# Half-width pairs: letting 128-column matmuls join the column tiling of their neighbours, with a new hand-searched order

## The chip, the cores and the metric

The kernel runs on one core of one Trainium2 chip. The core has a matmul engine (TensorE, "PE" in the profile; its weight loads stand apart as "PEld"), VectorE (DVE), ScalarE (ACT), GpSimd (POOL), and SyncE (SP), which here issues DMAs. Matmuls write to PSUM, eight banks of 128 partitions by 512 float32. The metric is the device time of one launch in microseconds (us). Times of the kernel before are the median of three runs.

## The reference, cut to what matters

Two identical layers, each an attention with a recurrent memory followed by a gated feed-forward net (FFN). Sizes: 2048 tokens of width 576, 32 heads of 128, segments of 32 tokens, 8 memory tokens, FFN width 4608. All in bfloat16.

```python
def _A_ref(x, mem0, Wq, Wk, Wv, Wo, seg_len):
    ...
    for s in range(n_seg):                       # 64 segments, in sequence
        xs = x[:, s * seg_len:(s + 1) * seg_len, :].copy()
        h = jnp.concatenate([mem, xs], axis=1)   # 8 + 32 = 40 rows
        q = jnp.einsum('btd,dhe->bhte', h, Wq)
        k = jnp.einsum('btd,dhe->bhte', h, Wk)
        v = jnp.einsum('btd,dhe->bhte', h, Wv)
        scores = jnp.einsum('bhqe,bhke->bhqk', q, k) * scale
        scores = jnp.where(mask[None, None], scores, -1000000000.0)
        p = _softmax(scores, axis=-1)
        o = jnp.einsum('bhqk,bhke->bhqe', p, v)
        o = jnp.einsum('bhte,hed->btd', o, Wo)
        mem = o[:, :M, :].copy()                 # the next segment needs it
        outs.append(o[:, M:, :])
...
x = x + _A_ref(_layernorm(x, axis=-1), A_mem0, A_Wq, A_Wk, A_Wv, A_Wo, A_seg_len)
x = x + _B_ref(_layernorm(x, axis=-1), B_w1, B_w3, B_w2)   # silu(x w1) * (x w3), then w2
x = x + _A_ref(_layernorm(x, axis=-1), A_mem0, A_Wq, A_Wk, A_Wv, A_Wo, A_seg_len)
x = x + _B_ref(_layernorm(x, axis=-1), B_w1, B_w3, B_w2)
```

The memory makes the 64 segments of a layer a chain: a segment's keys and queries cannot be computed until the output projection of the segment before is done.

## The kernel before, in words

**Steps.** The second layer's weights are the first's, so the kernel runs both layers at once, the second eight segments behind (`LAG`). A step `t` handles segment `t` of layer 0 and `t-8` of layer 1, 80 rows in all; there are 72 steps, and in the first and the last few only one layer is there (40 rows). Wq, Wk, Wv and Wo stay in SBUF (`W`, `WV`, `WO`); the FFN's weights are streamed for each group of four segments through small buffers (`W13`, `W2C`), 18 "pairs" of 256 FFN columns per group. At the end W and WV are no longer needed, and the last group's FFN weights are loaded straight into them (`tail_load`).

**Nodes and letters.** `make_nodes` describes the whole program as nodes: an engine, an assumed duration, dependencies, and slots of buffer pools that it takes and gives back. The order of the PE nodes is written out by hand as a string with one letter per node (`FIRST`, then `FOUR` eleven times, each for four steps, then `LAST`). The letters: Q and q are the projection to q and k and its remainder (576 = 4 x 128 + 64; lower case is always the 64-row remainder), S the scores, T the transposes of the probabilities (matmuls against an identity), P probabilities times V, O and o the output projection and the remaining 64 of its 576 columns, V, X, G (v, x, g) the passes that make V for memory rows, for segment rows, and for both kinds of rows in 128 columns, F and f the FFN's first half, W and w its second half for layer 0 and layer 1, and m, a, b, n, p transposes around the layer norms and residuals.

**The plan.** `plan` walks through that string and gives the instructions of the other engines their order by assumed durations: a node starts when its engine, its inputs and its slots are free; ACT and DVE share the "AD" nodes (PSUM copies), the first free takes one. The order in each queue is fixed then; the chip waits on semaphores.

**Tilings of the PE array.** Each PE node has a `mode`. "full" uses the array as one of 128 rows by 128 columns. "row" splits it in two of 64 rows (q, f, g: two remainders side by side). "col" splits it in two of 64 columns (S of two layers, o). "c32", "oct" and "quad" split it in 32-column strips, those by 64 rows, and four quarters (V, X and v, x). In `plan` every change of mode between neighbours in the string costs the assumed `SWITCH` = 0.098 us. The emitter writes matmuls through `mm` (line 580 of the profile), ACT operations through line 583, DVE's through line 586, and SP's DMAs through line 589, so all PE groups in the profile bear L580.

Of the kernel before, what the change touches and what calls it, by code (L numbers as in the profile page):

```python
# [13 lines left out]
P = 128  # L14
R64 = 64
# [36 lines left out]
class Node:  # L52
# [3 lines left out]
    def __init__(self, eng, dur, fn, deps=(), prio=0.0, mode=None, acq=(), rel=(), name="", lat=None):  # L56
        self.eng, self.dur, self.fn, self.prio, self.mode = eng, dur, fn, prio, mode
        self.deps = [d for d in deps if d is not None]
        self.acq, self.rel, self.name = list(acq), list(rel), name
        self.lat = lat if lat is not None else (PE_LAT if eng == "PE" else EW_LAT)  # L60
        self.outs, self.ready, self.start, self.end, self.by = [], 0.0, None, None, None
        self.left = len(self.deps)
# [13 lines left out]
def plan(nodes, pools, letters):  # L76
# [16 lines left out]
    mode = None  # L93
    order = []
    at = 0
# [18 lines left out]
    while len(order) < len(nodes):  # L114
        best = None
        for e in t_eng:
            if e == "PE":
                cands = seq[at:at + 1] if at < len(seq) and seq[at].left == 0 else []
            else:
                cands = ready[e] + (both if e in ("ACT", "DVE") else [])  # L120
            if not cands:
                continue
            ests = [(est(e, n), n) for n in cands]
            t = min(x for x, _ in ests)
            if t >= NOW:
                continue
            if best is None or t < best[0]:
                best = (t, e, ests)
        if best is None:
            raise RuntimeError(f"the plan is stuck at {at}: {seq[at].name}")  # L130
        t, e, ests = best
        st, n = min((x for x in ests if x[0] <= t + 1e-9), key=lambda x: x[1].prio)
        dur = n.dur
        if isinstance(dur, tuple):
            dur = dur[0] if e == "ACT" else dur[1]
        if e == "PE":
            at += 1
            if n.mode != mode:
                dur += SWITCH
                mode = n.mode  # L140
        elif n.eng == "AD":
            both.remove(n)
        else:
            ready[e].remove(n)
        n.start, n.end, n.by = st, st + dur, e
        t_eng[e] = n.end
        for s in n.acq:
            if s.i is not None:
                continue
            f = free[s.pool]  # L150
            s.i = min((i for i in range(len(f)) if f[i] <= st + 1e-9), key=lambda i: f[i])
            f[s.i] = NOW
        for s in n.rel:
            s.users -= 1
            s.end = max(s.end, n.end + (PE_LAT if e == "PE" else EW_LAT))
            if s.users == 0:
                free[s.pool][s.i] = s.end
        for m in n.outs:
            m.ready = max(m.ready, n.end + (0.0 if m.eng == e == "PE" else n.lat))
            m.left -= 1  # L160
            if m.left == 0:
                push(m)
        order.append(n)
    return order
# [20 lines left out]
def ewh(*ns):  # L185
# [5 lines left out]
    "maQqqqQQSQqqqQTQSqqQSQSXVxvPTPTOPOTOoooPOoQQQqqVSqqvQQqqSQQqqSQTXPSxTOPTPOTOPoooOoaQQqqqqQSvQVSqQQqTQSqqQSPTPOOT"  # L191
    "ooPTPOOooQQqqqvqSVQQQqSTQqqQPSqQOSoTXPTOPTOPxooOoQQpQqqqqQSVSnvqQFffqFQQTSqqPQOToSfFPWTOPfFTOPFOfoooWQQfqqqQSvVF"
    "qfQFQWSqqQFSfQTQPqqfFOTSoWPFTOPfxXTFPOOoooWQQqqfqQQSfqFSvVfqqQFQWSqTQQPFqffTOSoPWOTFPFTOPfaOoooWQFQqqfQSVvqqfFQQ"
    "SqWQQqqqQSTPSTbOPoXTOPTxxPOOoooXqqQpQQqqSVvnQFFSfqQqfqQQTSqfFPQTOPSofWTOPFOTFPWOoooFQqqffQQqSQQQqqgqGTSWPQQfqqFF"
    "fgSSTGGPFgfTOWPOfgGTOPFOooooWQQfqqqFQvSfqFQQfqSVTFQqfFQPSaTWQPfqqFOSoTWFOPffFTOPWOoooFQqqqfQQSWQqqQQSqqTbQSGgqgQ"
    "PGTGPSggOTGPOTOPoooOoQQppqqVqqvSQQnnQFSfqfqFTQQPFSqqfQTwOPWFSoffTOFPwTOPWOoooFQffqqFQwWSQQFfqqfFTGqqgSQPQFWTQSgf"
    "qqGQwPFTSfggOGGPOTwPOOooooWFfqqQQFQqfqvVSQQWFfqqSQwTFPaSqfqQTQwFWPSffTOPFOOTwPWOooooFqqfqQQWqSQQQSqqqQQbQSqggGTG"
    "PGTSggPGTOPOTwPOOoooo"
)
FOUR = (  # L200
    "QqQpQpQqqqvVSSnnQFffqqFQQTFSffqqQPFTWSPOwTFPOTOPwOooooWQQqqqfQSQQQqqqfFGgfSSTFPFQqfqgGQTWwPFTSfggGFPGOTOPOOooooW"
    "wQQqqqfQFQvfqfVSSwFQWQFqffqFWTQPwTFSffqqQOPWoSwTFPFOTOPwWOoooffFQqqQWQSqqqQaQSbQQTQqqqgGSSgPGTGPOTggGPOTwPOOoooo"
)
LAST = (
    "QQpqqqQpSqqQQnVqvSnQTQQPqqSFTSffOPFOTFPfwTOPFOooooWQQqfqqQFwWSfqfQQFGSgfqqQTFPGwSTWFqfgqQQPWTFSfgfgGFwGPOTOPOOoo"
    "oofFWQwQFqfqqQQWSfqVvSQFTFqqfQPQTwSqqfFOQPWwffSFTFPOOTFPWOoooowQQqqqfQQSvqqqVSQWTQQPqqQOTSSbPwvVoXTOPToxPOOooVpp"
    "qqvQQQqqSQQnnQqqfSFQTFPSfqqQTFfSPOOwTWPFfTOPFOoooowQWfqqQQQFvqqfVSSFQQfqqFTWQfqqSQPwTOPoSXfTFPOWOTxfPFOwoooFQQvq"
    "fqVSqqQQWwFTQqfqfSQQPFwFqfqSQTWOPSfFTFWPOTOPwOooooffQFqqQWQSqqqQwFvSfVQTQPWqqQSOQqwTSbPOTXoPToxPOOooQqqqqQpQQSVv"
    "QnqSQFqfqfFQTQqSPSwTOPFFTffoPOTOPwOoooFQqqfqQQqfvSVFQFQSqfqQTQQqfqSFPSXTwPOTFPOTxooPOOoowQQqqvfSVqqqQQQSqQQTSfFP"
    "FTfqqQOoSPwTfOFPFTOPfooOowQQqqqqQSQQSqfqFQVvSfFTwQQqfqPTSFPFTOPOTOPwOooooffpFnwFfffFFFwffFFwfffFFwFwfffFFFwfffFF"  # L210
    "wFwFffffFFww"
# [11 lines left out]
def make_nodes(em, nseg, pools, o=Opt, dma_bw=230e3, load_bw=400e3):  # L223
# [44 lines left out]
    def ln_nodes(tag, src, xn, deps, prio, writes, warm=False):  # L268
# [5 lines left out]
        d = node("PE", 5 * 0.056, em.ln_tr(xn, b, warm), deps=[c], prio=prio, mode="full", acq=[b], rel=[xn], name=tag + "tr")  # L274
# [26 lines left out]
    def v_nodes(name, t, k, prio, tail_at, emit, strips, deps, tail_deps, free):  # L301
# [6 lines left out]
        for r in (0, 1):  # L308
            outs = em.v_parts(strips, r)
            b[r].users = len(outs)  # L310
            for p0, width, row, blk in outs:
                e = node("AD", ew(512), em.v_ev(b[r], p0, width, row, blk), deps=[m_, n] + free.get(blk // 2, []), prio=prio + 0.01 * (blk // 2),
                         rel=[b[r]], name=name + "e")
                vx_ev.setdefault((name, t, blk // 2), []).append(e)
# [6 lines left out]
    def vg_nodes(t, g, deps, tail_deps):  # L321
# [4 lines left out]
        m_ = node("PE", 8 * 0.2158, em.vg(t, g, b, False), deps=deps, prio=t + o.vm, mode="full", acq=b, name="VG")  # L326
# [5 lines left out]
    def vg_out(t, g, b, deps, row):  # L332

        return [node("AD", ew(512), em.v_ev(b[r], row, R64, row, 2 * g + r), deps=deps, prio=t + o.vm + 0.01 * g + (0.05 if row == 0 else 0.0), rel=[b[r]],
# [11 lines left out]
    def step(t):  # L346
# [17 lines left out]
        for g in range(NG):  # L364
# [18 lines left out]
            sc = node("PE", 8 * 0.0165 * nl, em.scores(t, g, qs, s), deps=qe, prio=pf + o.sc, mode="col", acq=[s, sme], rel=qs, name="SC")  # L383
# [9 lines left out]
            tr = node("PE", 8 * mm80, em.ptr(t, g, pb, bt), deps=[pbs], prio=pf + o.tr, mode="full", acq=[pts] + bt, name="TR")  # L393
            node("POOL", 1.2, em.pb_zero(pb), deps=[tr], prio=pf, rel=[pb], name="pbz")
            pe_ = [node("AD", ew(4 * c80), em.pt_ev(t, g, m, bt[m], pts), deps=[tr], prio=pf, rel=[bt[m]], name="PTe") for m in (0, 1)]
            if paired(t):
# [6 lines left out]
                      prio=pf + o.pv, mode="full", acq=b + [ot], rel=[pts], name="PV")  # L403
# [14 lines left out]
        if t == nst - 1:  # L418
            last_reads[2].extend(wos)
# [14 lines left out]
    def post(li, g):  # L434
# [4 lines left out]
                 prio=prio, mode="full", acq=b, name="POST")  # L439
# [3 lines left out]
    last_reads = [], [], []  # L443
    kept = {}

    def job(j):
# [18 lines left out]
        if last:  # L465
            v_done, qk_done, wo_done = last_reads
            tail = []
            for i in range(8):
                late = wo_done[i - 4:i - 3] if i >= 4 else []
                parts = [(0, 9 * 512, qk_done[2 * i:2 * i + 2] + late), (1, 4 * 576, v_done + late)]  # L470
                tail.append([load("tail", kb(128, c), s0 + o.tail_at + 0.01 * i, em.tail_load(i, what), deps=dep) for what, c, dep in parts])

        npp = NPR // 2
        for at, pp in enumerate([npp - 1] + list(range(npp - 1)) if last else range(npp)):
            mids, w2s, htts, lds = [], [], [], []
            stays = last and pp == npp - 1
            for pr_ in (2 * pp, 2 * pp + 1):
# [18 lines left out]
                fm = node("PE", 16 * mm, em.ffn_up(ents, pr_, w13, b, last and not stays, False), deps=wr + ld, prio=prio, mode="full",  # L496
# [8 lines left out]
            for (bi, g) in ents:  # L505
                b = banks()
                d = node("PE", 8 * 0.1225, em.ffn_down(bi, pp, htts, w2s, b, last and not stays), deps=mids + lds, prio=prio + o.w2,
                         mode="full", acq=b, rel=htts + w2s, name="W2b" if bi else "W2")
# [52 lines left out]
class Emitter:  # L561


    def __init__(self, nc, tc, T, aps, nseg):
# [4 lines left out]
        self.tail_w, self.ys = {}, {}  # L569
# [9 lines left out]
    def mm(self, out, lhsT, rhs, start, stop, **k):  # L579
        self.ch("PE", self.nc.tensor.matmul(out, lhsT=lhsT, rhs=rhs, start=start, stop=stop, skip_group_check=True, **k))  # L580
# [113 lines left out]
    def tail_load(self, i, what):  # L694

        def f(n):
            T = self.T
            fa = i * 512
            t13, t2 = T.W[:, :, fa:fa + 512], T.WV[:, i * 4 * D:(i + 1) * 4 * D].rearrange("p (b d) -> p b d", b=4)
            if what != 1:  # L700
                for kind, wd in ((0, self.a.w1), (1, self.a.w3)):
                    self.dma(t13[:, 4 * kind:4 * kind + 4], wd[0:4 * P, fa:fa + 512].rearrange("(c p) f -> p c f", p=P))
                for kind, wd in ((0, self.a.w1), (1, self.a.w3)):
                    self.dma(t13[kind * R64:(kind + 1) * R64, 8], wd[4 * P:D, fa:fa + 512])
            if what != 0:
                self.dma(t2, self.a.w2[fa:fa + 512, :].rearrange("(b p) d -> p b d", p=P))
            for h in range(2):
                self.tail_w[2 * i + h] = (t13[:, :, h * 2 * P:(h + 1) * 2 * P], t2[:, 2 * h:2 * h + 2])
# [219 lines left out]
    def scores(self, t, g, qs, s):  # L928

        def f(n):  # L930
            S = self.bk(s)[:, 0:GH * QW].rearrange("p (h k) -> p h k", h=GH)
            both = self.both(t)
            for hl in range(4):
                for ab in (0, 1):
                    Q = self.T.QKT[:, qs[ab].i].rearrange("p a h n -> p (a h n)")
                    for kd in ((0, 1) if both else (0,)):
# [3 lines left out]
                                True, True, tile_position=(0, 64 * kd))  # L940
# [249 lines left out]
def kernel(  # L1190
# [88 lines left out]
    for n in plan(nodes, pools, ORDER):  # L1279
        n.fn(n)  # L1280
# [35 lines left out]
```

## Time and profile before

| what | value |
|---|---|
| median of 3 runs | 2701.53 us (2697.99 to 2702.61) |
| the profiled execution's own time | 2696.12 us |
| its span, first to last instruction | 2694.4 us |
| granted TensorE clock | 0.995 of full speed |
| PE busy | 98% of the span, 55,795 matmuls |
| DVE / ACT / POOL busy | 78% / 51% / 12% |
| DMA | 321 MB, 119 GB/s on average |

The profile's matmuls are pipelined: one matmul's record lasts about 0.2 us, but the next may start 0.036 us after it, so PE counts as busy even when little is done. What an operation costs is therefore read from starts: from the start of its first matmul to the start of the first matmul of whatever follows. In a timeline, the columns are the start in us, the length of a merged group in us, the engine and line, the operation, its output and inputs, its shape and the number of instructions. "128\*64" ahead of a shape means 128 rows and 64 columns of weights; "128\*128" is the full array.

### The profile page before, as it was taken

The numbers are of one execution on the slowest core, as the hardware profiler recorded it, in microseconds if no ns is written. First come the engines' busy times: TensorE is split into PE (matmuls) and PEld (weight loads), VectorE is DVE, ScalarE is ACT, GpSimd is POOL, SyncE is SP. The second block draws the span as 40 slices with busy tenths as digits, with TensorE's granted clock in tenths as the row PEclk, the third lists the DMA queues.
The fourth block names the chain that finished last, engine by engine and source line by source line (L and its number), as shares of the span: only waits on it lengthen the run. The fifth ranks groups of instructions, "written<-read, shape, count | busy, mean of one in ns | idle before, by whom it ended". The sixth has DMA issues, their size and how long they took to land.

```text
span 2694.4 us, 126628 instructions
## 1 busy us (share of the span) xinstructions
PE 2635.1 (98%) x55795; PEld 2225.2 (83%) x55795; DVE 2088.9 (78%) x5376; ACT 1366.8 (51%) x4025; POOL 333.2 (12%) x400
## 2 busy tenths in 40 slices
PE   5999999999999999999999999999999999999998
PEld 4788888888888888888888888888888888888886
DVE  4777887878778777777877777787787777787876
ACT  2655554545545454554545445464544546454453
POOL 1111110111101011010101101010110101011110
PEclk8999999999999999999999999999999999999999
DMA  9064524234342423434243343433334342434458
GB/s 317 8 188 126 159 79 120 81 110 119 108 134 71 126 84 110 124 106 131 76 119 89 110 126 97 129 88 114 94 110 126 92 133 71 125 97 135 119 161 263
DMA packets 483065, 321.42 MB, mean 119 GB/s; under 512 B 26344, under 2 KB 477296, under 8 KB 481872
## 3 DMA queue, kind: packets, MB, share of 16 engines
q1 hardware_dynamic: 478976, 305.44, 38.5%
q8 instruction: 437, 7.16, 1.1%
q0 software_dynamic: 3024, 6.93, 0.9%
q10 hardware_dynamic: 512, 0.94, 0.1%
q14 instruction: 116, 0.95, 0.1%
HBM read 308.49 MB, written 2.36 MB: 115 GB/s over the span
## 4 chain that ended last, share of the span: by engine, by line
PE 88%; ACT 4%; DMA 3%; DVE 3%; issue 1%; SPq 0%; ACTq 0%; POOL 0%; DVEq 0%; POOLq 0%
PE bank L580 88%; ACT V L583 3%; DMA W<-in_B_w_dram 2%; DVE SME L586 1%; DMA W<-in_A_Wk_dram 1%; DVE STAT L586 1%; DVE V L586 1%; ACT SME L583 0%; DMA WV<-in_A_Wv_dram 0%; ACT XTB L583 0%; ACT QKT L583 0%; ACT PTS L583 0%; SPq L589 0%; DVE PB L586 0%; DVE OT L586 0%
## 5 line engine op out<-in xcount | busy, mean ns | idle before, releaser
L580 PEld LDWEIGHTS <-W 128*128 128x128 bf16 (+1 forms) x29520 | 1237.5, 98 | 141.9 <-issue 44.3
L580 PE MATMUL bank<-HT,W 128*128 128x80 bf16 (+3 forms) x23040 | 810.9, 196 | 17.0 <-ACT HT L583 6.3
L580 PE MATMUL bank<-XTB,W 128*128 128x256 bf16 (+3 forms) x6480 | 660.9, 261 | 6.7 <-DMA W<-in_B_w_dram 5.9
L583 ACT ACTIVATE QKT<-bank 128x256 bf16<-128x256 f32 (+3 forms) x1587 | 365.9, 317 | 369.1 <-PE bank L580 350.0
L995 POOL MEMSET PB<- 128x1024 bf16 x288 | 273.9, 951 | 1809.8 <-PE bank L580 1312.3
L580 PE MATMUL bank<-OT,WO 128*128 128x80 bf16 (+3 forms) x11520 | 406.8, 198 | 0.8 <-DVE OT L586 0.5
L583 ACT ACTIVATE V<-bank 64x512 bf16<-64x512 f32 (+1 forms) x616 | 346.4, 584 | 105.9 <-PE bank L580 100.6
L580 PEld LDWEIGHTS <-WO 128*128 128x128 bf16 (+1 forms) x11520 | 379.4, 102 | 15.9 <-issue 5.8
L580 PE MATMUL bank<-WV,HT 128*32 128x512 bf16 (+4 forms) x3240 | 367.5, 383 | 1.0 <-issue 0.7
L580 PE MATMUL bank<-W2C,HTT 128*128 128x288 bf16 x2240 | 315.1, 286 | 0.0
L586 DVE TENSOR_TENSOR PB<-SME,STAT 40x128 bf16<-40x128 f32 (+4 forms) x912 | 275.2, 336 | 14.9
L586 DVE TENSOR_REDUCE STAT<-SME 104x8 f32<-104x320 f32 (+1 forms) x576 | 273.5, 475 | 14.5 <-ACT SME L583 9.3
L583 ACT ACTIVATE HTT<-bank 128x512 bf16<-128x512 f32 (+1 forms) x324 | 179.7, 556 | 181.8 <-PE bank L580 179.8
L580 PEld LDWEIGHTS <-HT 128*32 128x32 bf16 (+4 forms) x3240 | 136.9, 96 | 152.3 <-issue 33.4
L586 DVE SCALAR_TENSOR_TENSOR XR<-bank,XR 128x288 f32<-128x288 f32 x576 | 246.2, 449 | 16.0 <-PE bank L580 8.0
L580 PEld LDWEIGHTS <-HTT 128*128 128x128 bf16 x2304 | 209.7, 98 | 48.5 <-DVE HTT L586 0.3
L583 ACT ACTIVATE OT<-bank 128x320 bf16<-128x320 f32 (+1 forms) x399 | 149.5, 404 | 166.1 <-PE bank L580 165.0
L586 DVE CAST QKT<-bank 128x192 bf16<-128x192 f32 (+2 forms) x461 | 124.7, 316 | 134.3 <-PE bank L580 133.0
L586 DVE SCALAR_TENSOR_TENSOR HTT<-HTT,bank 128x512 bf16<-128x512 bf16 (+1 forms) x324 | 202.1, 624 | 33.7 <-ACT HTT L583 29.7
L586 DVE TENSOR_TENSOR HTT<-HTT,bank 128x512 bf16<-128x512 bf16 (+1 forms) x324 | 203.4, 628 | 30.7 <-DVE HTT L586 0.5
L583 ACT ACTIVATE PTS<-bank 128x320 bf16<-128x320 f32 (+1 forms) x384 | 144.1, 402 | 163.4 <-PE bank L580 126.7
L583 ACT ACTIVATE SME<-SME 104x320 f32<-104x320 f32 (+1 forms) x288 | 135.4, 470 | 138.3 <-DVE SME L586 135.6
(61 smaller groups left out, 1803.3 us busy)
## 6 DMA issues: line engine op xcount, KB each, us to landing
W<-in_B_w_dram SPq DMA_DIRECT2D x612, 256.0 KB, 3.5
W2C<-in_B_w_dram SPq DMA_DIRECT2D x306, 288.0 KB, 3.3
W<-in_B_w_dram SPq DMA_DIRECT2D x612, 32.0 KB, 3.4
W<-in_B_w_dram SPq DMA_DIRECT2D x16, 512.0 KB, 8.8
W<-in_A_Wq_dram SPq DMA_DIRECT2D x9, 512.0 KB, 9.0
WO<-in_A_Wo_dram SPq DMA_DIRECT2D x4, 1152.0 KB, 15.3
XR<-in_A_x_dram POOLq DMA_DIRECT2D x16, 288.0 KB, 2.9
WV<-in_B_w_dram SPq DMA_DIRECT2D x8, 576.0 KB, 7.1
```

The source lines that it names most:

```text
L580: self.ch("PE", self.nc.tensor.matmul(out, lhsT=lhsT, rhs=rhs, start=start, stop=stop, skip_group_check=True, **k))
L583: self.ch("ACT", self.nc.scalar.activation(*a, **k))
L586: self.ch("DVE", getattr(self.nc.vector, fn_)(*a, **k))
L995: return lambda n: self.ch("POOL", self.nc.gpsimd.memset(self.T.PB[:, pb.i], 0.0))
```

## The change

**Modes become lists.** A node may name several modes ("full/col"). FFN (F, W, w), the 128-column V passes (G), the transposes (T, p, n, a, b) and P may run in either; Q, O and m stay "full"; the scores of a single layer, which need only 40 columns, may also be either. While the planner walks along the string it keeps the modes that all nodes since the last change have in common, and changes only when the next node shares none of them. The run of nodes then takes the first mode that is left (`settle`): "full" unless a neighbour in the run is only "col".

**Pairs.** In mode "col", `mm` splits a 128-column matmul into two of 64 columns, at column 0 and column 64 of the array, each with the same moving operand.

**The assumed costs** of copying V out of PSUM and of a single layer's scores are new constants.

**The tail's loads.** The last group's FFN weights come in four loads of 1024 FFN columns instead of eight of 512, and the later ones no longer wait for output projections.

**The order strings** `FIRST`, `FOUR` and `LAST` are all new, of the same letters and lengths.

```diff
-        self.eng, self.dur, self.fn, self.prio, self.mode = eng, dur, fn, prio, mode
+        self.eng, self.dur, self.fn, self.prio, self.mode = eng, dur, fn, prio, mode.split("/") if mode else mode
...
-    mode = None
+    mode, run = [], []
...
+    def settle():
+        for x in run:
+            x.mode = mode[0]
+        run.clear()
...
-            if n.mode != mode:
+            if not any(m in mode for m in n.mode):
                 dur += SWITCH
+                settle()
                 mode = n.mode
+            mode = [m for m in mode if m in n.mode]
+            run.append(n)
...
-            sc = node("PE", 8 * 0.0165 * nl, em.scores(t, g, qs, s), deps=qe, prio=pf + o.sc, mode="col", acq=[s, sme], rel=qs, name="SC")
+            sc = node("PE", 8 * (0.0165 * nl if nl == 2 else 0.029), em.scores(t, g, qs, s), deps=qe, prio=pf + o.sc, mode="col" if nl == 2 else "full/col", acq=[s, sme], rel=qs, name="SC")
...
-        m_ = node("PE", 8 * 0.2158, em.vg(t, g, b, False), deps=deps, prio=t + o.vm, mode="full", acq=b, name="VG")
+        m_ = node("PE", 8 * 0.2158, em.vg(t, g, b, False), deps=deps, prio=t + o.vm, mode="full/col", acq=b, name="VG")
...
(the same for the nodes TR, PV, FF, W2, POST and the layer norms' transposes)
...
-            for i in range(8):
-                late = wo_done[i - 4:i - 3] if i >= 4 else []
-                parts = [(0, 9 * 512, qk_done[2 * i:2 * i + 2] + late), (1, 4 * 576, v_done + late)]
-                tail.append([load("tail", kb(128, c), s0 + o.tail_at + 0.01 * i, em.tail_load(i, what), deps=dep) for what, c, dep in parts])
+            for i in range(4):
+                parts = [(0, 9 * 1024, qk_done[4 * i:4 * i + 4]), (1, 8 * 576, v_done)]
+                tail += [[load("tail", kb(128, c), s0 + o.tail_at + 0.01 * i, em.tail_load(i, what), deps=dep) for what, c, dep in parts]] * 2
...
     def mm(self, out, lhsT, rhs, start, stop, **k):
+        if self.mode == "col" and "tile_position" not in k:
+            for r in (0, R64):
+                self.mm(out[r:r + R64], lhsT[:, r:r + R64], rhs, start, stop, tile_position=(0, r), **k)
+            return
         self.ch("PE", self.nc.tensor.matmul(out, lhsT=lhsT, rhs=rhs, start=start, stop=stop, skip_group_check=True, **k))
...
     for n in plan(nodes, pools, ORDER):
+        em.mode = n.mode
         n.fn(n)
```

## The prediction

> **What bounds the kernel now.** I read the page first.
>
> ```profile
> PE 2635.1 (98%) x55795; PEld 2225.2 (83%) x55795; DVE 2088.9 (78%) x5376; ACT 1366.8 (51%) x4025; POOL 333.2 (12%) x400
> PEclk8999999999999999999999999999999999999999
> PE 88%; ACT 4%; DMA 3%; DVE 3%; issue 1%; SPq 0%; ACTq 0%; POOL 0%; DVEq 0%; POOLq 0%
> ```
>
> PE carries the chain; the rest sits mostly at the two ends, where weights arrive. "98% busy" does not say what the time goes to, so I read the PE timeline for starts.
>
> ```profile
> 1107.11 1.15 PE L580 MATMUL bank<-W2C,HTT 128*128 128x288 bf16 x8
> 1108.18 0.34 PE L580 MATMUL bank<-OT,WO 128*64 128x80 bf16 x8
> 1108.35 0.41 PE L580 MATMUL bank<-QKT 128*64 128x40 bf16 x16
> 1108.69 0.54 PE L580 MATMUL bank<-W2C,HTT 128*128 128x288 bf16 x3
> ```
>
> Full tiling, then column tiling (o and S), then full again. W2 took 1.07 from its start to o's. Where no change of tiling follows, it takes 0.98:
>
> ```profile
> 1503.71 1.15 PE L580 MATMUL bank<-W2C,HTT 128*128 128x288 bf16 x8
> 1504.69 2.00 PE L580 MATMUL bank<-OT,WO 128*128 128x80 bf16 x64
> 1506.63 1.15 PE L580 MATMUL bank<-W2C,HTT 128*128 128x288 bf16 x8
> ```
>
> So a change cost 0.09 here. Over all the trace's starts, from the last matmul of one tiling to the first of another, it is 0.132 to 0.134 after an 80-column matmul (0.036 without a change) and 0.202 to 0.205 after a 256-column one (0.109 without): 0.093 to 0.098, I take **0.097**. Walking the order string with the rule for modes, the kernel before changes tiling 1,294 times, or 125 us. By the same starts some 2,465 us are matmuls at their full rate. The rest is waiting: about 2.5 us in each 200 us of the middle, but some 31 us in the first 100 us and 14 in the last 95.
>
> **Part 1, changes of tiling removed.** One turn of `FOUR`, a bar for each change, before and after:
>
> ```
> |Q|q|QpQpQ|qqq|v|V|SS|nnQF|ffqq|FQQTF|S|ffqq|QPFTW|S|POwTFPOTOPwO|oooo|WQQ|qqqf|Q|S|QQQ|qqqf|FG|gf|SS|TFPFQ|qfqg|GQTWwPFT|S|fgg|GFPGOTOPOO|oooo|WwQQ|qqqf|QFQ|v|fqf|V|SS|wFQWQF|qffq|FWTQPwTF|S|ffqq|QOPW|oS|wTFPFOTOPwWO|ooo|ff|FQ|qq|QWQ|S|qqq|QaQ|S|bQQTQ|qqqg|G|SS|g|PGTGPOT|gg|GPOTwPOO|oooo
>
> |Q|qq|v|pQQpQ|qq|V|SSnn|QQF|ffqq|FQTQ|qqf|SFPwTWFS|ff|OPFTWPOTOPwO|ooooF|qfqq|QQQWQ|q|wSSFF|ffgq|GQTQPQ|gqqq|GTwS|QPWG|SFT|fgfg|FPGOTOPOwO|ooooF|qffq|QFQWQ|q|S|V|v|QQQ|qqqf|FTWPwSSFF|qffq|QQTOw|SWPFT|ff|FOPWTwPOO|ooooF|qqfq|QQQWQ|S|qqq|aQ|S|QQbQ|gqq|SGTSGP|g|TGPOT|gg|GPOTOPwO|oooo
> ```
>
> That is 65 against 57, eleven times; `FIRST` goes from 320 to 274, `LAST` from 259 to 209. Together 1,294 to 1,110: 184 fewer. Eight of them lie where loads set the pace (six in step 0, two in the tail after the last p), so 176 x 0.097 = **-17.1 us** on the path. Nothing else runs on PE at a change, so nothing hides it.
>
> **Part 2, the pairs.** By the same walk 166 of 324 F, 104 of 288 W and w, 43 of 108 G, 62 P, 89 T and 30 transposes become pairs: 5,190 added matmuls, each with a weight load. If a pair costs what the one matmul did, this is free; 17.1 us over 5,190 pairs is 3.3 ns, so that is the margin. The trace has pairs of four kinds. At 512 columns, first the full form (8 matmuls), then two-column tiles (8 pairs):
>
> ```profile
> 1455.48 1.89 PE L580 MATMUL bank<-WV,HT 128*128 128x512 bf16 x8
> 1457.21 0.45 PE L580 MATMUL bank<-ident,PB 104*128 104x80 bf16 x8
> ```
>
> ```profile
> 2391.70 1.92 PE L580 MATMUL bank<-WV,HT 128*64 128x512 bf16 x16
> 2393.46 0.40 PE L580 MATMUL bank<-QKT 128*64 128x40 bf16 x16
> ```
>
> 1.73 against 1.76: 4 ns a pair, and by the single starts (0, 240, 456, 671 ns ...) all of it in the first pair. At 80 columns, the 64 matmuls from 1504.69 to 1506.63 above are 32 O and 16 pairs of o: 1.94 - 32 x 0.036 - 2 x 0.097 = 0.60, 37 ns a pair against 36. At 40 columns it is worse, 30 against 25:
>
> ```profile
> 1004.71 0.68 PE L580 MATMUL bank<-QKT 128*64 128x40 bf16 x32
> ```
>
> (0.68 - 0.19 for the last one) / 31 = 16 ns a matmul. Only 17 of the new nodes (8 T, 9 P) are that short: 17 x 8 x 5 ns = +0.7 us. Pairs of 256 and 288 columns the trace doesn't show; they lie between 80 and 512, so 0 to +4 ns each: 3,488 pairs, 0 to +14 us. I take +0.3, for the excess in the rows sits at the first pair of a node. In all **+1**, with ends 0 and +15.
>
> [...]
>
> **Part 3, waits that the new order makes or ends.** PE's queue is in order: a node that waits holds up all behind it. I summed the PE work between each producer and its consumer in `FOUR`, and compared it with the shortest distance that ran without a wait in the trace. Scores to T has 6.35 at least (ran at 5.27), V to P 2.1 (1.8), F to w 5.4 (4.0), T to P and P to O 0.98 as before. Three, once in each turn, are shorter than any seen: o to p 2.07 (2.83 seen), q to S 1.34 (1.74), b to g 1.24 (1.81). What p needs after o:
>
> ```profile
> 1506.76 0.22 ACT L583 ACTIVATE HT<-bank 128x64 bf16<-128x64 f32 x1 [2.56 <-PE bank L580]
> 1507.01 0.23 ACT L583 ACTIVATE YO<-bank 64x80 f32<-64x80 f32 x1
> 1507.28 0.35 DVE L586 TENSOR_TENSOR HT<-bank,YO 64x16 bf16<-64x16 f32 x2 [1.87 <-ACT YO L583]
> 1507.66 0.45 ACT L583 ACTIVATE YTS<-bank 128x128 bf16<-128x128 f32 x2 [0.41 <-DVE HT L586]
> 1508.51 0.28 DVE L586 TENSOR_TENSOR YTS<-bank,YO 64x32 bf16<-64x32 f32 x2
> ```
>
> Done at 1508.79, 2.3 after the last o (1506.53, 0.036 after its last start); 0.4 of that is DVE being elsewhere. So p waits 0 to 0.3, and the other two alike: 33 x (0 to 0.3) = 0 to +10. On the other side, each turn before (157.5 us) holds waits of 0.41 (Q after o, which stays), 0.39 (inside a q) and 0.28 (inside a P); the last two may vanish, 11 x 0.67 = -7. I take **+2** (-7 to +10). DVE, at 78%, keeps its work; 0.5% less time does not make it the bound.
>
> **Part 4, the ends.** The tail waits for weights:
>
> ```profile
> 2678.69 0.84 PE L580 MATMUL bank<-XTB,W 128*128 128x128 bf16 x12 [1.28 <-DMA W<-in_B_w_dram]
> 2684.43 3.83 PE L580 MATMUL bank<-XTB,W 64*128 64x128 bf16 x40 [2.69 <-DMA W<-in_B_w_dram]
> ```
>
> With one of 0.8 at 2685, the excess at these places is 5.1 us. The same bytes now come in 20 DMAs on SP's queue instead of 40, in rows of 2 KB instead of 1 KB, and without waiting for O. At best all waits go: -5. At worst the last load lands when it did (2685.8) and, now holding twice the columns, has 4 F, 4 f and 2 w behind it (6.3 us by rows) where before 4.6 followed: +2. A load of the small W2 buffer waits in the same queue (issued at 2647.7) and still holds back what is behind it. I take **-1.5**. At the start, V's matmuls ended at 44.9; the last of Wv landed at 42.4 and a quarter of them must follow, so at best 43.7: **-1** (0 to -1.2).
>
> **The sum.** -17.1 + 1 + 2 - 1.5 - 1 = -16.6 against the profiled execution's own 2696.1, so 2679.5. That execution was 5.4 us under the median of 2701.5; against the median it is **2684.9**. The ends together, not all at once, give the forecast's own range of 2674 to 2697.
>
> **The rivals.**
>
> *The waits eat it.* The new distances cost 1.5 us a turn instead of 0.2, or the W2 and V copies queue up on ACT and DVE. For it: the order is tuned on assumed durations, and three distances are untested. Against it: the others are as long as before. 11 x 1.5 = 16.5, so about 2699, no change that counts.
>
> *A pair is not one matmul (slower).* One mechanism: with 64-column weight loads, the short pairs (T, P) run at the weight load's pace in longer runs than o's eight. Their place is the 1,208 pairs of T and P; it decides from 14 ns a pair (17 us) on. At 60 ns a pair (24 more) they cost 29 us, so 2684.9 + 29 = 2714. Against it: the o rows, where 16 pairs in a row ran at 37 ns. For it: no row has long columns between short pairs, and a margin of 3.3 ns over all pairs is thin.
>
> *The change isn't made:* the runs fall back to "full". The rule of `settle` counted above leaves 494 pair nodes, so I give this almost nothing (2701).
>
> **Chances.** Forecast 0.82, waits 0.09, pairs 0.08, not made 0.01. What a measurement of this kernel can tell from no change is about 0.2%, or 5.4 us. The forecast lies wholly beyond it but for its upper end (0.01 of it): faster 0.81, same 0.11 (0.09 + 0.01 + 0.01), slower 0.08. The range of 2673 to 2699 takes in the forecast's ends and reaches to the waits' case.
>
> **What would show it.** In the profile after: about 61,000 matmuls; groups of 128\*64 for XTB, W2C, PTS and PB; F nodes in pairs that still take 1.75 us, W2 0.98, T and P 0.29 from start to start; a turn of `FOUR` of some 156.8 us instead of 157.5; the two waits for W in the tail shorter. Wrong would be: pairs of T or P over 50 ns, more than 1 us of new waits a turn before p, S or g, or an end that waits longer for W.

## The result, and the profile after

| | median | ratio to before (95%) |
|---|---|---|
| before, beside it | 2702.07 us (2697.99 to 2704.96, 4 runs) | |
| after | 2691.87 us (2686.26 to 2696.43, 4 runs) | 0.9962 [0.9939, 0.9986] |
| the same kernel again (e1) | 2694.26 us (2686.84 to 2696.46, 9 runs) | 0.9973 [0.9964, 0.9983] |

Faster by 7 to 10 us by the two ratios; the forecast was 16.6. The profiled execution of after took 2696.43 us, near the top of its range, that of before 2696.12, below all its timed runs; so the two traces must be compared stretch by stretch, not by their ends. From after's page:

```profile
PE 2622.5 (97%) x60931; PEld 2286.7 (85%) x60995; DVE 2103.0 (78%) x5463; ACT 1361.9 (51%) x3938; POOL 332.5 (12%) x400
PEclk8999999999999999999999999999999999999999
q8 instruction: 477, 7.82, 1.2%
PE 85%; DVE 7%; DMA 3%; ACT 2%; issue 1%; SPq 1%; POOL 0%; ACTq 0%; DVEq 0%
```

60,995 weight loads are the 55,795 of before, 5,190 of the pairs and 10 of a warm-up node in pairs (64 matmul records are missing in this trace). The third line is what the prediction left out: 477 instruction packets with 7.82 MB, 16.4 KB each. Before had 437 with 7.16 MB.

The pairs in the timeline of after (start, length, group; twice as many matmuls in each):

```profile
1490.58 1.94 PE L591 MATMUL bank<-XTB,W 128*64 128x256 bf16 x32
1492.33 0.48 PE L591 MATMUL bank<-PTS,V 128*64 128x80 bf16 x16
1492.62 1.17 PE L591 MATMUL bank<-W2C,HTT 128*64 128x288 bf16 x16
1493.60 0.48 PE L591 MATMUL bank<-ident,PB 104*64 104x80 bf16 x16
1493.88 1.18 PE L591 MATMUL bank<-W2C,HTT 128*64 128x288 bf16 x16
1494.87 1.94 PE L591 MATMUL bank<-XTB,W 128*64 128x256 bf16 x32
```

From start to start F takes 1.75, P 0.29, W 0.98, T 0.28, W 0.99: what they took in the full array. At these sizes a pair costs what the one matmul did.

Where the time went shows best in four stretches: first Q to the first `FOUR` (FIRST), the eleven turns (middle), from there to the last p (LAST), and the tail to the last matmul. "Pauses" are gaps that end 1.15 to 1.8 us after an instruction packet's landing, where every instruction delivered before it had been used. A packet lands when its 16.4 KB have arrived. All from starts in the traces, us; the kernels e1 to e12 are those of the experiments.

| trace | FIRST | middle | LAST | tail | pauses in FIRST / LAST |
|---|---|---|---|---|---|
| before | 502.0 | 1734.1 | 392.2 | 40.0 | 3.0 / 3.2 |
| after | 508.1 | 1722.8 | 397.0 | 39.6 | 7.3 / 4.8 |
| e1, after again | 504.7 | 1724.9 | 398.1 | 39.4 | 5.9 / 5.9 |
| e5, only the middle changed | 505.2 | 1725.0 | 396.1 | 40.3 | 4.6 / 4.1 |
| e6, only the ends changed | 504.2 | 1737.6 | 399.3 | 38.4 | 4.6 / 7.7 |
| e7, old tail loads | 502.6 | 1723.4 | 397.5 | 39.6 | 5.8 / 5.7 |
| e12, LAST old | 500.2 | 1723.5 | 395.3 | 45.3 | 4.0 / 4.7 |
| e8, before, no repeated loads | 502.0 | 1732.3 | 393.4 | 35.3 | 2.3 / 4.5 |
| e9, ends, no repeated loads | 496.5 | 1733.4 | 402.3 | 35.9 | 0.4 / 7.0 |
| e10, after, no repeated loads | 495.6 | 1720.5 | 402.9 | 36.2 | 1.3 / 8.9 |

The middle gained 9 to 11 us, more than forecast for it. The ends, where I had counted half of the removed changes of tiling, gained nothing.

**Why the ends had fewer changes to remove.** A score of a single layer has weights of 40 columns. The changed kernel calls 62 of the 64 such nodes "full" and gives them no place in the array; I counted no change around them. In the trace of after, and then in that of before, where the same node is called "col":

```profile
154.61 0.37 PE L591 MATMUL bank<-QKT 128*40 128x40 bf16 x8
154.92 0.34 PE L591 MATMUL bank<-HT,W 128*128 128x40 bf16 x7
157.88 0.78 PE L591 MATMUL bank<-HT,W 128*128 128x40 bf16 x25 [2.62 <-issue]
```

```profile
2626.29 0.37 PE L580 MATMUL bank<-QKT 128*40 128x40 bf16 x8
2626.59 0.94 PE L580 MATMUL bank<-HT,W 128*128 128x40 bf16 x31
```

0.31 and 0.30 from the score's first matmul to Q's first. Eight matmuls of the same 40 moving columns with 128-column weights, in e1's trace, take 0.21:

```profile
2616.61 0.35 PE L591 MATMUL bank<-PTS,V 128*128 128x40 bf16 x8 [0.35 <-ACT PTS L594]
2616.82 1.14 PE L591 MATMUL bank<-W2C,HTT 128*128 128x288 bf16 x8
```

So leaving a "full" score still costs a change. So does entering it: from the last matmul of a Q of 40 columns to the first score it is 109 ns in the median in before (20 nodes called col) and 109 in e7 (21 called full), against 25 from one Q to the next. Leaving takes about 111 under either name, so around these scores a change costs some 85 ns. And in the one place where o, which is in two-column tiling, follows a "full" score, there is no such gap: in a further trace of after (span 2688.9 us) the first o starts there at 114.63 us, ahead of the last two scores (114.65). So the gaps go by the width of the weights here, not by the node's name: in the programs that the two kernels build, the 512 matmuls of these scores carry the same tile, 128 rows by 64 columns at column 0, whichever name the node has.

Counted with these scores in column tiling, `FIRST` has 320 changes before and 311 after, the middle 715 and 627, `LAST` 259 and 259: **97 fewer, not 184**, 88 of them in the middle.

**What a pause drags behind it.** The last line of the first of these fences is the other surprise: 2.62 us in the middle of a Q node that waits for no data. It costs more than its length: right behind it the same 20 FFN matmuls take 1.81 us to the next start (first two lines) and 1.10 in e10, where the pause is missing (last two):

```profile
158.50 2.01 PE L591 MATMUL bank<-XTB,W 128*128 128x128 bf16 x20
160.31 0.47 PE L591 MATMUL bank<-HT,W 64*128 64x40 bf16 x16
```

```profile
152.88 1.27 PE L592 MATMUL bank<-XTB,W 128*128 128x128 bf16 x20
153.98 0.36 PE L592 MATMUL bank<-HT,W 64*128 64x40 bf16 x16
```

The further trace of after shows the clock at such a place: 1.00 from 2620 to 2625 us, then a pause (2.34 us for instructions, to 2628.0), a granted clock of 0.50 from 2629.8 to 2640.0 (with a second pause in it, of 1.19) and 1.00 again from 2641 to 2646. Not every pause is followed by it: behind one of 1.84 us (to 211.0) the clock stays at 1.00 in the same trace, behind one of 2.07 us (to 2635.2) in a further trace of before (span 2695.6 us). A stretch of 3.4 us at half clock costs up to 1.7 us, which the table's pauses leave out.

### The profile page after: what moved, and what is told of

Same layout as the page of the kernel before. It is cut to its first block, busy times and chain, and to the rows that moved or that the text cites. A ratio compares the mean times of both kernels' runs of the same rounds, so it can differ in the third digit from the quotient of the medians.

```text
span 2694.7 us, 137011 instructions
## 1 busy us (share of the span) xinstructions
PE 2622.5 (97%) x60931; PEld 2286.7 (85%) x60995; DVE 2103.0 (78%) x5463; ACT 1361.9 (51%) x3938; POOL 332.5 (12%) x400
## 3 DMA queue, kind: packets, MB, share of 16 engines
q1 hardware_dynamic: 474048, 305.43, 38.4%
q8 instruction: 477, 7.82, 1.2%
## 4 chain that ended last, share of the span: by engine, by line
PE 85%; DVE 7%; DMA 3%; ACT 2%; issue 1%; SPq 1%; POOL 0%; ACTq 0%; DVEq 0%
PE bank L591 85%; DVE STAT L597 1%; ACT V L594 1%; DVE SME L597 1%; DVE HTT L597 1%; SPq L600 1%; DMA W<-in_B_w_dram 1%; DVE PB L597 1%; DMA W<-in_A_Wk_dram 1%; DVE V L597 1%; DVE XN L597 0%; DMA WO<-in_A_Wo_dram 0%; DVE LNS L597 0%; DMA XN<-in_A_x_dram 0%; ACT PTS L594 0%
## 5 line engine op out<-in xcount | busy, mean ns | idle before, releaser
L591 PEld LDWEIGHTS <-W 128*128 128x128 bf16 (+2 forms) x32176 | 1267.8, 100 | 130.0 <-issue 62.6
L591 PE MATMUL bank<-XTB,W 128*64 128x256 bf16 (+5 forms) x9136 | 659.3, 263 | 5.6 <-DMA W<-in_B_w_dram 3.7
L594 ACT ACTIVATE QKT<-bank 128x64 bf16<-128x64 f32 (+2 forms) x1500 | 349.7, 312 | 352.7 <-PE bank L591 347.1
L591 PE MATMUL bank<-W2C,HTT 128*64 128x288 bf16 (+1 forms) x3072 | 323.6, 287 | 1.4 <-DMA W2C<-in_B_w_dram 1.0
L591 PEld LDWEIGHTS <-HT 128*32 128x32 bf16 (+5 forms) x3584 | 154.2, 98 | 124.8 <-issue 17.4
L591 PEld LDWEIGHTS <-HTT 128*64 128x64 bf16 (+1 forms) x3136 | 223.7, 105 | 35.7 <-issue 2.4
L594 ACT ACTIVATE OT<-bank 128x320 bf16<-128x320 f32 (+1 forms) x420 | 155.2, 403 | 147.6 <-PE bank L591 144.6
L597 DVE CAST QKT<-bank 128x128 bf16<-128x128 f32 (+4 forms) x548 | 147.6, 316 | 87.9 <-PE bank L591 85.6
## 6 DMA issues: line engine op xcount, KB each, us to landing
W<-in_B_w_dram SPq DMA_DIRECT2D x8, 1024.0 KB, 12.3
```

The lines of the kernel that those rows point to most:

```text
L594: self.ch("ACT", self.nc.scalar.activation(*a, **k))
L597: self.ch("DVE", getattr(self.nc.vector, fn_)(*a, **k))
```

## The experiments

Three theories at first: (A) instructions come late, (B) the new ends wait longer for data, (C) short pairs cost more. That "full" scores change the tiling came out of the traces last.

**e1, the changed kernel again.** No edit.

> The kernel after, unchanged, for a tighter interval and a second profile. Three theories of why the gain was 10 us and not 17. (A) Instructions arrive late: the pairs add 9% to PE's instructions, and where 40-row steps need one matmul per 25 ns PE now and then runs out of them. Then the long pauses inside Q nodes of the first profile (1.1, 2.8 and 2.2 us at 150, 155 and 214 us, 2.5 and 1.4 at 2631 and 2638) move or change length from run to run, each with a packet of PE's instruction queue that starts late, and the times scatter by some 10 us. (B) The new FIRST and LAST wait longer for data: the same waits stand at the same nodes with the same lengths. (C) Short pairs cost more than one matmul: the middle turns lose it, 44 nodes of P and 66 of T. All three: ratio 0.994 to 0.999.

The gain is there again: 2694.26 us, 0.9973. In the table its middle is as in after, and pauses sit at the same stages with other lengths: the Q at 155 us paused 2.6 us in after and 1.7 in e1.

**e2, the new modes on the old strings; e3, the new strings without pairs.**

```diff
 e2: FIRST, FOUR, LAST of before, all else as after
 e3:
-mode.split("/") if mode else mode
+mode.split("/")[:1] if mode else mode
-mode="col" if nl == 2 else "full/col"
+mode="col"
```

> The new modes, pairs, assumed costs and tail loads on the old order strings: 1,210 changes of tiling instead of 1,294, 286 nodes with pairs (or wide V) instead of 498. By the count alone 84 x 0.097 = 8.1 us faster than the kernel before, 2694. (A) fewer added instructions, so less is lost than after: 2692 to 2698. (B) the old strings have the old waits: the whole 8 us, plus or minus the tail. (C) P and T pairs are 84 instead of 151 nodes: a loss of 0.05 us each at their ends would leave 4 us of the gain.

> The new order strings with one mode to a node, as before (everything of 128 columns in full tiling, all scores in column tiling), so no pairs: 1,412 changes of tiling. By the count 118 x 0.097 = 11.4 us slower than the kernel before (2713) and 302 x 0.097 = 29 us slower than the kernel after (2721), as the new strings were made for pairs. (A) PE's instructions are as many as before, so its long pauses are as short as before (about 4 us): nearer to 2710. (B) the waits of the new strings stay, whatever the tiling: 2718 or more. (C) faster than the count by what the pairs cost.

e2: 2723.16 us, ratio 1.0093 [1.0079, 1.0108]. e3: 2742.65 us, 1.0156 [1.0142, 1.0169]. Both far slower than before, and than anything I expected of them. The waits of e3, then of e2:

```profile
PE bank L591 <- ACT V L594: 15.3, 34, 2.1
PE bank L591 <- DVE HTT L597: 7.6, 23, 0.5
PE bank L591 <- DVE PB L597: 7.4, 8, 1.9
```

```profile
PE bank L591 <- ACT V L594: 9.3, 26, 2.9
PE bank L591 <- DVE PB L597: 8.0, 10, 1.8
PE bank L591 <- DMA W2C<-in_B_w_dram: 5.3, 3, 3.9
```

(us in all, times, longest. In before V's row is 5.2 and PB's 1.4, and HTT has none.) A string, its modes and its assumed costs fix the order of every queue together; these rows fit that one without the others queues V's and P's copies in the wrong places. These two say nothing of a change's price, but they show that the parts' worths don't add up.

**e4, pairs for Q and O too.**

```diff
-  ... mode="full", ... name="QK")      (and name="WO")
+  ... mode="full/col", ...
```

> The kernel after with Q and O allowed in column tiling as well: 881 changes of tiling instead of 1,110, and 1,537 nodes with pairs instead of 498, some 25,500 added matmuls instead of 5,190. By the count 229 x 0.097 = 22 us faster than after: 2669. (A) PE's instruction queue must bring 46% more than before, and an 80-column pair uses up four instructions in 36 ns: PE waits for instructions in the middle turns too, and the time is over 2700. (B) nothing new waits: 2670 to 2680, less what the plan's fixed order loses. (C) at 1 ns or more a short pair 20 us or more of the gain go.

2949.47 us, 1.0919 [1.0903, 1.0936]. Its waits, and a Q stretch of its timeline:

```profile
PE bank L591 <- issue: 187.7, 210, 2.7
...
567.34 2.48 PE L591 MATMUL bank<-HT,W 128*64 128x80 bf16 x128 [0.81 <-issue]
571.09 0.81 PE L591 MATMUL bank<-HT,W 128*64 128x80 bf16 x35 [1.26 <-issue]
```

At 80 columns the pairs still run at the single's rate (a Q node of pairs 1.14 to 1.17 us); at 40 they don't (1.14 against 0.81). But 128 matmuls with their 128 weight loads are one packet of 256 instructions; PE used this one up in 2.5 us and then stood for 1.26. C falls at 80 columns, A is real.

**e5, only the middle changed; e6, only the ends; e7, the old tail loads.** Each hybrid takes the strings, modes and V costs of before in the steps named; e5 has the old tail loads, e6 the new.

```diff
 in plan, e5 (e6 without the "not"; with the strings and V costs to match):
+    for i, n in enumerate(seq):
+        if not len(FIRST) <= i < len(FIRST) + 11 * len(FOUR):
+            n.mode = n.mode[:1]
 e7:
-            for i in range(4):
+            for i in range(8):
+                late = wo_done[i - 4:i - 3] if i >= 4 else []
```

> The middle eleven turns as in the changed kernel (order, pairs, assumed copy costs), both ends (FIRST, LAST, the tail's loads) as before; 1,206 changes of tiling against 1,294 and 1,110. Between the two profiled runs the eleven turns gained 11.3 us. If the ends are where the rest of the forecast gain is lost (late instructions there, theory A, or waits for data there, theory B), this kernel keeps all of the 11.3: ratio to before 0.9958, about 2689 us, as fast as the changed kernel or some 3 us faster, with pauses without a data wait summing to about 9 us as before. If the middle's gain only moves a wait from the middle to the last part (rival D), the gain shrinks to under 6 us (ratio over 0.9978).

> The ends (FIRST, LAST, the tail's loads) as in the changed kernel, the eleven middle turns as before; 1,198 changes of tiling, 96 fewer than before, 88 of them on the path. By the price of a change alone: -8.5 us, -1.5 for the tail, -1 for the head, so ratio 0.9959 (2689). Theories A and B: the ends' new order loses what it saves to late instructions (A) or to waits for data (B), so -2 to +4 us, ratio 0.9993 to 1.0015. A shows in the trace as pauses inside nodes with no data wait, summing to 12 to 15 us against 9 before, at other nodes in each execution; B as waits on ACT, DVE or DMA at the same nodes each time, 4 us or more above before's.

> The changed kernel with the tail's weight loads as before: 40 transfers of 1 KB rows instead of 20 of 2 KB, the last four pieces held back until O is done. The prediction's term for this was -1.5 us (bounds -5 to +2), so undoing it should cost +1.5: ratio to the changed kernel 1.0006. By the two profiled runs the tail gained 0.4 us: then no difference (0.9998 to 1.0004). If 2 KB rows keep the queues so busy that instructions come late near the end (A at the tail), undoing it is a gain of 1 to 3 us.

e5: 2690.65 us, 0.9965 [0.9954, 0.9976], as fast as the whole change. e6: 2704.74 us, 1.0012 [1.0004, 1.0021], slower by 3 us. e7: 2691.6 us, 0.9965 [0.9953, 0.9977], no difference. The whole gain is the middle's. The ends bring nothing: of the 88 changes that I had counted on the path there, 9 are real. The tail takes 39.6 us in after and in e7, so its term is not seen either. The waits at the tail of after are smaller but more:

```profile
2658.61 0.40 PE L591 MATMUL bank<-W2C,HTT 128*128 128x288 bf16 x2 [0.58 <-DMA W2C<-in_B_w_dram]
2672.63 0.23 PE L591 MATMUL bank<-XTB,W 64*128 64x128 bf16 x1 [0.69 <-DMA W<-in_B_w_dram]
2682.47 0.84 PE L591 MATMUL bank<-XTB,W 128*128 128x128 bf16 x12 [1.80 <-DMA W<-in_B_w_dram]
```

**e8, e9, e10, e11: before, e6, after and e4 without the FFN's repeated weight loads.**

```diff
 in load_w13 (load_w2 alike):
+            if w13.i in self.seen13:
+                return
+            self.seen13.add(w13.i)
```

> The kernel before without the FFN's repeated weight loads (each slot of W and W2C is loaded once, the tail's loads stay; the FFN then computes with the wrong weights). The traffic beside PE's instruction packets is gone in the body. Theory A (instructions come late because the packets share the queues' engines with the weight loads): the pauses with no data wait, 9 us in the trace of before, fall under 3 us, and the few waits for W (about 2 us) go: ratio to before 0.996 to 0.997. If a packet is late for reasons of its own, the pauses stay at 9 us and the ratio is 0.998 to 1.000.

> The kernel whose ends alone are changed (e6), again without the FFN's repeated weight loads; to be set against the same edit of before (e8). With the loads the ends' change cost 3.7 us. Theory A: with the loads gone the 88 removed changes of tiling come through, e9 is 6 to 9 us faster than e8, and both traces hold under 3 us of pauses. Theory B (the new order of the ends waits for data on ACT and DVE): e9 is within 3 us of e8, since these waits need no DMA.

> The changed kernel without the FFN's repeated weight loads. Theory A: e8 minus 15 to 18 us, the forecast sum, since nothing holds up the instructions. Theory B: e8 minus 7 to 11 us, as with the loads.

> Every full node may pair (e4: 25,500 more matmuls, 2,949 us with 242 us of pauses for instructions), without the FFN's repeated weight loads. If the packets are late only through the weight loads, most of the pauses go and the time falls to 2,690 to 2,760 us. If the fetch itself can't keep up with a matmul each 16 to 18 ns, 2,900 us or more stay.

(Each buffer of W13 and W2C is loaded once, so most of the FFN works on the wrong weights; the tail's loads stay.) e8: 2691.14 us (2690.77 to 2691.62), 0.9963 [0.9949, 0.9977]. e9: 2694.91 us, 0.9977 [0.9968, 0.9986]. e10: 2683.65 us, 0.9933 [0.992, 0.9947]. e11: 2859.41 us, one run.

e8's time is what A forecast, but not for A's reason: its pauses in the ends are 6.8 us against 6.2 in before, and what its trace gains is 4.7 us in the tail and 1.8 in the middle. In FIRST theory A holds: PE's waits from 60 to 530 us in after and then in e10 differ by more than 0.3 us in one row alone (three rows of each),

```profile
PE bank L591 <- issue: 6.5, 7, 2.6
PE bank L591 <- ACT PTS L594: 1.3, 4, 0.4
PE bank L591 <- DVE PB L597: 1.0, 1, 1.0
```

```profile
PE bank L592 <- ACT PTS L595: 1.3, 4, 0.4
PE bank L592 <- DVE PB L598: 1.0, 1, 1.0
PE bank L592 <- issue: 0.3, 2, 0.2
```

and the Q that paused at 155 us now runs through:

```profile
151.76 0.37 PE L592 MATMUL bank<-QKT 128*40 128x40 bf16 x8
152.06 0.97 PE L592 MATMUL bank<-HT,W 128*128 128x40 bf16 x32
```

The new FIRST is then 5.5 to 6.4 us shorter than the old, about half of it in step 0, while weights still arrive; with the loads, in five traces, it is between 1.8 shorter and 6.1 longer than the old one in before (which itself takes 3.2 more in e5). Its 9 changes are 0.9 us of that; the rest is shorter pauses, waits and stretches at half clock.

But e9 is still 3.8 us slower than e8, against A's expectation, and e10 only 7.5 faster, as B said: LAST takes 402 us instead of 393. Instructions come late there (pauses 7.0 and 8.9 against 4.5) while the tail's loads, which stay, run: in e10 the packet that this Q waits for starts with one instruction left, and the transfers around it move 375 GB/s:

```profile
2623.93 0.87 PE L592 MATMUL bank<-HT,W 128*128 128x40 bf16 x28 [2.81 <-issue]
```

And part of LAST runs slower: 16 F take 1.59 us from 2640.57 on in e9, behind a pause of 2.84, and 0.89 from 2624.53 on, ahead of it. LAST holds four such stretches at half clock in e9 (three of them behind a pause), three in e10 and none in e8, up to 6.8 and 5.1 us more. The rows of waits for data (over 0.15 us) sum to 5.5 and 6.3 us against 3.5; with the loads to 5.1 to 6.3 in the four traces of the new LAST and 3.4 to 5.3 in the three of the old. So of LAST's 9 us without the loads most is late instructions and the half clock behind them, and 2 to 3 us are longer waits for data (B); the new LAST saves no change of tiling for either. e11 falls between its two forecasts and keeps most of e4's loss:

```profile
PE bank L592 <- issue: 121.6, 173, 3.8
```

**e12, the changed kernel with the old LAST.**

```diff
+    for i, n in enumerate(seq):
+        if i >= len(FIRST) + 11 * len(FOUR):
+            n.mode = n.mode[:1]
 (LAST, and the V costs and scores from step 60 on, as before)
```

> The changed kernel with the last eight steps as before (the string LAST, its single modes and assumed costs; 1,160 changes of tiling against 1,110, +4.9 us by their price); FIRST, the middle and the tail's loads as changed. Without the repeated weight loads the steps after the middle and the tail together took 428.7 us in the order of before and 438.2 and 439.1 in the new one, with them 432.2 against 436.4 to 437.7. Theory B for this part (the new LAST waits for data between 2,398 and 2,575 us whatever the loads do): LAST and tail take 431 to 434 us in this trace, and the time is 3 to 6 us under the changed kernel's 2,691 to 2,694: ratio to before 0.9945 to 0.9960. If the loss there is only late instructions (A), which differ from run to run, the part takes 435 to 438 us and the time is the changed kernel's or 1 to 2 us over it, ratio 0.9965 to 0.9980.

2696.01 us (2691.74 to 2697.75, 11 runs), 0.998 [0.9971, 0.9989]: not faster, if anything 2 to 4 us slower than the whole change. LAST is some 2 us shorter than in after, though by the names it has 50 more changes (4.9 us), and the tail gives it back threefold (LAST and tail 440.6 us together, outside both forecasts):

```profile
2665.47 4.73 PE L594 MATMUL bank<-XTB,W 64*128 64x128 bf16 x52 [4.17 <-DMA W<-in_B_w_dram]
2677.73 0.84 PE L594 MATMUL bank<-XTB,W 128*128 128x128 bf16 x12 [2.82 <-DMA W<-in_B_w_dram]
```

The body ends 8 us earlier than in after and then waits for the tail's weights. That the larger pieces, landing late as a whole, are to blame, and that LAST and the tail's loads are tuned to each other, fits these rows but is not shown. My expectation missed it.

No run made the single-layer scores 128 columns wide, the direct test of the miscount: 62 nodes and 87 changes, so at 85 ns each 7.4 us at stake. It is what I would try next, and whether the waits and pauses of the ends would leave any of it stays open.

## Why the prediction was right, and where not

The sign, the mechanism and the range held; the size was double what came.

- **Part 1, changes removed:** the price of 0.097 held (some 85 ns around scores of 40 columns), the number did not. The step that failed is "walking the order string with the rule for modes": it counts names, and 62 scores keep their column tiling under the name "full". 97 x 0.097 = 9.4 us in place of 17.1. The 7.7 between them are the size of the miss (16.6 against 7 to 10); the errors of the other terms, the middle's better and the ends' worse, nearly cancel, which is luck. A smaller slip: of the eight changes set apart, the strings give five in step 0, and behind the last p there are two more than before, not two fewer, so the miscounted term would be 181 x 0.097 = 17.6. The trace of before could have warned: a score is written 128\*40 there, no form of the full array.
- **Part 2, pairs:** taken at +1. Within a run they cost nothing from 80 columns on (F 1.750 against 1.750, T 0.286 against 0.288, P 0.284 against 0.286). Leaving a run costs a little more from a short pair: T to a row tiling 0.437 against 0.386 from the full array (25 nodes), P 0.451 against 0.385 (13), the transposes n to full 45 ns more (12). 1.3 + 0.9 + 0.5 = 2.7 us, within the ends 0 to +15. Pairs of 80 columns run at 18 ns a matmul.
- **Part 3, waits of the middle:** taken at +2, ends -7 and +10. The middle gained 9.1 to 11.3 in five traces with the loads; less 88 x 0.097 = 8.5 for the changes and some 2 for the exits, the waits fell by 3 to 5. Turns took 156.3 to 157.5 us, forecast 156.8.
- **Part 4, the ends:** tail -1.5 and head -1 taken; e7 shows no gain at the tail, and the first Q starts at 22.0 before and at 22.1 to 22.9 in the five traces with the new start and the loads. Missing from the working altogether were the late instructions, 6.2 us of pauses in the two ends of before and 11.5 to 12.3 in those of the four traces with both ends new and the loads, and the half clock behind some of them. The waits that I read "inside a q" and "inside a P" of the middle were waits of the order, as I took them: they stand in all eleven turns of before and in none of after, where S after f and O after P wait 0.34 and 0.28 instead.
- **The rivals:** "a pair is not one matmul" fell by the pairs of after and, in long runs, of e4, which keep the single's rate from 80 columns on. "The waits eat it" was right in kind for the ends, but there was less to eat than I thought, and the waits were for instructions as much as for data.

## What to carry to other kernels

Count changes of tiling by the width of the weights in the trace, not by what the program calls them: here scores with 40 columns of weights had 109 ns ahead of them and some 111 behind them under either name, where 25 is the pace without a change. Where matmuls are short, look at the instruction packets and ask whether a packet lasts as long as the next one takes to come (2.3 us against 3.25 in e11); behind a long pause, look at the granted clock too (0.50 from 2629.8 us on in the further trace of after). An order tuned on assumed costs is one piece with them: parts of it put back alone cost more than the whole change brought.

## What the runs showed of the hardware

- PE's instructions came in packets of 16.4 KB, 437 before and 477 after, of 256 instructions each: 111,590 matmuls and weight loads over 437 are 255, 121,990 over 477 are 256. In e10 the next packet started when some 245 were left (median); in the two further traces one took 1.03 to 1.04 us (medians). Pauses started where all delivered ones were used up (256 lie between the starts of two neighbouring ones, at 2625.5 and 2632.0 us in the further trace of after), and ended 1.15 to 1.8 us after the landing.
- At 40 columns 128 matmuls and their loads took 3.2 us (25 ns each), and packets that started late came too late. The packets that end after's pauses of 1.1 to 2.8 us at 150, 155 and 214 us start with 72, 0 and 18 instructions left, while transfers of 240 to 290 GB/s run. At 80 columns (36 ns each, 4.6 us) there is hardly such a pause: apart from e4 and e11 the middles of all traces hold one over 0.1 us, of 0.7 us (e2). Even without the repeated loads two packets never started less than 3.25 us apart in e11, while 128 matmuls of 18 ns use one up in 2.3: there PE waited 121.6 us for instructions, 173 times.
- The runs scatter less without the repeated loads: 10 us between the fastest and the slowest of after with them, 3 without (e10); 7 and 0.9 for before (e8). That the pauses, which differ from run to run, account for it is not shown: e8's trace still holds 6.8 us of them.
- Behind some of the pauses the granted clock was at half: 0.50 from 2629.8 to 2640.0 us in the further trace of after, behind 2.34 us without instructions; behind 1.84 us (after, to 211.0) and 2.07 us (before, to 2635.2) it was 1.00. What decides between them is not shown.
